# Earlier first products, joined input loads and 384/256 output pieces in a state-space and feed-forward kernel on one core

## The chip, the cores and the metric

The kernel runs on one core of a Trainium2 chip. The metric is the time of one execution on the device, in microseconds (us); less is better. A quoted time is the median of several executions, with the lowest and the highest in brackets. All times inside a trace count from the start of that execution's span; the timed execution is about 1.8 us longer than the span.

## The reference, cut to what matters

Two branches share the input `x` (2048 rows of 640 numbers, bf16) and are blended with a gate that is computed from each row.

```python
# cut: set-up of the inputs, types
x = A_x                                                   # (1, 2048, 640)
g = sigmoid((x * gate_w).sum(-1, keepdims=True))
# branch A: a diagonal complex state-space recurrence with input and output projections
Bu = einsum("bld,pd->blp", x, B_bar);  h = Lam_bar * h + Bu[:, t];  y = 2 * einsum(h, Cmat).real + x * Dskip
# branch B: a feed-forward block, 640 -> 1728 -> 640
b = gelu(x @ w1 + b1) @ w2 + b2
return g * a + (1 - g) * b
```

## The kernel before

The rows come in four chunks of 512; a chunk has four tiles of 128 rows (`TPC = 4`, `H = 2`, `P = 128`, `D = 640`). For the first chunk TensorE itself transposes `x`; the other chunks come by a transposing load. For each tile it first transposes columns 0 to 255 (I call this the tile's turn: two products against an identity matrix), and later the other 384 columns (its rest-turn: three products). The weights `w1` are split by columns into three blocks, `w1a`, `w1b` and `w1c`. The products with the first block, `w1a`, come in strips of six 128-column products, one per bank (a bank is one of the buffers that TensorE writes its products to), in between.

The first loads and their order of issue (cuts marked):

```python
load_x0(nc.sync, 0, 1, 0, KA * P)            # tile 0, columns 0..255
load_w1a(nc.scalar, 0)
load_x0(nc.sync, 1, 2, 0, KA * P)            # tile 1
load_w1a(nc.scalar, 1)
load_x0(nc.sync, 2, 3, 0, KA * P)            # tile 2
load_x0(nc.scalar, 0, H, KA * P, D)          # tiles 0 and 1, columns 256..639
load_x0(nc.sync, 3, 4, 0, KA * P)            # tile 3
load_w1a(nc.sync, 2)
# cut: two memsets on VectorE
warm = const.tile([P, 1], F32, name="warm")
nc.scalar.activation(out=warm[:], in_=nc.const_aps.tensor(1.0, [P, 1], BF16), func=ACT.Exp)
rows(nc.sync, prmA[0:KS, :], A_log_dt)       # a parameter row
rows(nc.sync, prmA[KS:2 * KS, :], A_Lambda_im)
rows(nc.sync, prmA[2 * KS:3 * KS, :], A_Lambda_re)
load_x0(nc.sync, H, TPC, KA * P, D)          # tiles 2 and 3, columns 256..639
# cut: the other weights (w1a rows 3 and 4, w1b, w1c, ...), all on nc.sync
```

TensorE's first work. The fillers multiply ones by ones and are thrown away; they are there so that the clock is raised soon.

```python
for n in (512, 512, 512, 512, 512, 512, 128, 128):
    nc.tensor.matmul(pA[:, 0:n], lhsT=ones(P), rhs=ones(n), start=True, stop=True)

def turn_first(a, other):
    t = bank()
    turn(t, 0, a, 0);          turned(nc.vector, t, 0, a, 0, 1)               # copied out by VectorE
    turn(other, a * P, a, 1);  turned(nc.scalar, other, a * P, a, 1, 2)       # copied out by ScalarE

turn_first(0, pA); turn_first(1, bank())
# cut
part(0, 0); part(0, 1)           # part(kd, a): strip kd on tile a, six products of 128 columns
turn_first(2, pA); part(1, 0); part(1, 1)
turn_first(3, pA); part(0, 2)
turn_rest(0, bank(), (nc.scalar, KA, KD)); part(1, 2)
# cut: a small product for the parameter rows, rest-turns of tiles 1, 2 and 3, all remaining strips,
# then full 512-column products with w1a, w1b, w1c
```

The down-projection of the feed-forward, whose 640 output columns the kernel spreads over two banks:

```python
MAIN, REST = (0, 512), (512, D)
# biased(): ScalarE fills a bank with the bias; two 128-column rests share a bank
# full():   13 products per tile and piece;   out_of(): ScalarE scales the piece out of the bank
```

Of the kernel before, what the change touches and what calls it, by code (L numbers as in the profile page):

```python
# [16 lines left out]
P = 128  # L17
T = 2048
D = 640
# [4 lines left out]
KS = D // P  # L24
# [3 lines left out]
TPC = CH // P  # L28
H = TPC // 2
# [12 lines left out]
def kernel(  # L42
# [19 lines left out]
    nc = tc.nc  # L62
# [12 lines left out]
    def bank(dtype=F32):  # L75
        return ps.tile([P, CH * 4 // (4 if dtype == F32 else 2)], dtype, name="bank")
# [19 lines left out]
    prmA = const.tile([P, P], BF16, name="prmA")  # L96
# [23 lines left out]
    def load_xn(c, a0=0, a1=TPC, queue=None):  # L120
        if a0 == 0:
            xn[c] = xnp.tile([P, TPC, D], BF16, name="xn")
        r0 = c * CH + a0 * P
        (queue or nc.sync).dma_start(out=xn[c][:, a0:a1, :], in_=x2d[r0:r0 + (a1 - a0) * P, :].rearrange("(a p) d -> p a d", p=P))

    def load_w1a(queue, kd):
        queue.dma_start(out=w1a[kd][:], in_=B_w1[kd * P:(kd + 1) * P, 0:cut1])

    def rows(queue, dst, v):
        queue.dma_start(out=dst, in_=v.rearrange("(j p) -> j p", p=P))  # L130

    KA = 2
    xn[0] = xnp.tile([P, TPC, D], BF16, name="xn")

    def load_x0(queue, a0, a1, d0, d1):
        queue.dma_start(out=xn[0][:, a0:a1, d0:d1], in_=x2d[a0 * P:a1 * P, d0:d1].rearrange("(a p) d -> p a d", p=P))  # L136
# [2 lines left out]
    load_w1a(nc.scalar, 0)  # L139
    load_x0(nc.sync, 1, 2, 0, KA * P)  # L140
    load_w1a(nc.scalar, 1)
    load_x0(nc.sync, 2, 3, 0, KA * P)
    load_x0(nc.scalar, 0, H, KA * P, D)
    load_x0(nc.sync, 3, 4, 0, KA * P)
    load_w1a(nc.sync, 2)
    nc.vector.memset(prmA[:], 0.0)
    nc.vector.memset(prmB[:], 0.0)
    warm = const.tile([P, 1], F32, name="warm")
    nc.scalar.activation(out=warm[:], in_=nc.const_aps.tensor(1.0, [P, 1], BF16), func=ACT.Exp)
    rows(nc.sync, prmA[0:KS, :], A_log_dt)  # L150
    rows(nc.sync, prmA[KS:2 * KS, :], A_Lambda_im)
    rows(nc.sync, prmA[2 * KS:3 * KS, :], A_Lambda_re)
    load_x0(nc.sync, H, TPC, KA * P, D)
# [36 lines left out]
    class Clock:  # L190
        pe = 3.4
        act = 12.0
# [8 lines left out]
    def let_out(until, chunk=-1):  # L201
        while pend:
            ready, cost, fn, _ = pend[0]
            start = max(ck.dve, ready)
            if start >= until and not any(x[3] == chunk for x in pend if chunk >= 0):
                return
            pend.pop(0)
            fn()
            ck.dve = start + cost
# [6 lines left out]
    def pe(cols):  # L216
        ck.pe += cols / 2400.0 + 0.002

    def act(cost):
        ck.act = max(ck.act, ck.pe + 0.2) + cost  # L220
        return ck.act
# [4 lines left out]
    nc.vector.tensor_copy(out=tf[:], in_=tfi[:])  # L226
    ones = lambda n: nc.const_aps.tensor(1.0, [P, n], BF16)
    pA = bank()
    for n in (512, 512, 512, 512, 512, 512, 128, 128):
        nc.tensor.matmul(pA[:, 0:n], lhsT=ones(P), rhs=ones(n), start=True, stop=True)  # L230

    def turn(p, col, a, kd):
        nc.tensor.matmul(p[:, col:col + P], lhsT=xn[0][:, a, kd * P:(kd + 1) * P], rhs=ident[:], start=True, stop=True,  # L233
                         skip_group_check=True)

    def turned(engine, p, col, a, k0, k1):
        dst = xT[0][:, k0:k1, a * P:(a + 1) * P]
        src = p[:, col:col + (k1 - k0) * P].rearrange("p (k t) -> p k t", t=P)
        if engine is nc.vector:
            nc.vector.tensor_copy(out=dst, in_=src)  # L240
        else:
            nc.scalar.activation(out=dst, in_=src, func=ACT.Identity)  # L242

    def turn_first(a, other):
        t = bank()
        turn(t, 0, a, 0)
        turned(nc.vector, t, 0, a, 0, 1)
        turn(other, a * P, a, 1)
        turned(nc.scalar, other, a * P, a, 1, 2)

    turn_first(0, pA)
    turn_first(1, bank())

    def col(name, dtype=F32, n=KS):
        return const.tile([P, n], dtype, name=name)
# [68 lines left out]
    banks = [bank() for _ in range(FA)]  # L324

    def strip(kd, t0, t1, first, f0=0, f1=FA):
        for kf in range(f0, f1):
            ff1_mm(banks[kf], 0, kf, kd, t0, t1, first, 3)
# [30 lines left out]
    def part(kd, a):  # L359
        strip(kd, a * P, (a + 1) * P, kd == 0)  # L360

    part(0, 0)
    part(0, 1)
    turn_first(2, pA)
    part(1, 0)
    part(1, 1)
    turn_first(3, pA)
    part(0, 2)
# [175 lines left out]
    def ssm(c, at={}):  # L544
        hs[c] = hsp.tile([P, 2 * KS, CH], BF16, name="hs")
        for ks in range(KS):
            if ks in at:
                at[ks]()
            bu = work.tile([P, 2, CH], BF16, name="bu", bufs=8)
            for ri, BT in enumerate((BT_re, BT_im)):  # L550
                p = bank()
                for kd in range(KD):
                    nc.tensor.matmul(p[:], lhsT=BT[ks >= KSA][:, kd, (ks % KSA if ks < KSA else ks - KSA) * P:][:, 0:P], rhs=xT[c][:, kd, :],  # L553
                                     start=(kd == 0), stop=(kd == KD - 1))
                    pe(CH)
                nc.scalar.activation(out=bu[:, ri, :], in_=p[:], func=ACT.Identity)  # L556
                act(0.6)
            scan_ops(c, ks, bu, ck.act)
            if c == 0 and ks == 0:
                later(0, 1.6, factors)  # L560
            let_out(ck.pe)
# [24 lines left out]
            dve_now(ck.pe, 0.45, lambda: nc.vector.tensor_tensor(out=p[:, 0:d1 - d0], in0=xn[c][:, a, d0:d1], in1=Dbc[:, d0:d1], op=ALU.mult))  # L586
            seeded[ti].append(p)

    MAIN, REST = (0, 512), (512, D)
    opened = {}  # L590

    def biased(c, kind, i):
        p = bank()
        d0, d1 = MAIN if kind == "wide" else REST
        n = 1 if kind == "wide" else H
        v, src = p[:, 0:n * (d1 - d0)], b2bc[:, d0:d1]
        if n > 1:
            v = v.rearrange("p (j d) -> p j d", j=n)
            src = src.rearrange("p (o d) -> p o d", o=1).to_broadcast([P, n, d1 - d0])
        nc.scalar.activation(out=v, in_=src, func=ACT.Identity)  # L600
        act(0.6 if n == 1 else 0.4)
        opened[c, kind, i] = p

    def first_banks(c):
        biased(c, "wide", 0)
        biased(c, "wide", 1)

    def fin_b(c, at={}):
        def full(p, col, a, d0, d1):
            for kf in range(KF - 1):  # L610
                nc.tensor.matmul(p[:, col:col + d1 - d0], lhsT=gel[c][:, kf, a * P:(a + 1) * P], rhs=w2_sb[:, kf, d0:d1],  # L611
                                 start=False, stop=False, skip_group_check=True)
                pe(d1 - d0)

        def out_of(p, col, a, d0, d1):
            ti = c * TPC + a
            if gbs[ti] is None:
                gbs[ti] = fwork.tile([P, D], F32, name="gb")
            nc.scalar.activation(out=gbs[ti][:, d0:d1], in_=p[:, col:col + d1 - d0], func=ACT.Identity, scale=gcol[:, 1, ti:ti + 1])  # L619
            act(0.7 if d1 - d0 > 320 else 0.4)  # L620

        def half_rows():
            for d0, d1 in (MAIN, REST):
                for j in range(H):
                    for h in range(2):
                        p, col = (opened[c, "wide", h * H + j], 0) if d0 == 0 else (opened[c, "rest", h], j * P)
                        nc.tensor.matmul(p[:, col:col + d1 - d0], lhsT=gelL[c % 2][h * F_LAST:(h + 1) * F_LAST, j, :],  # L627
                                         rhs=w2l[h * F_LAST:(h + 1) * F_LAST, d0:d1], start=False, stop=True, skip_group_check=True)
                    pe(d1 - d0)
            ck.pe += 0.2  # L630

        biased(c, "rest", 0)
        biased(c, "wide", 2)
        for h in range(2):
            for j in range(H):
                a = h * H + j
                full(opened[c, "wide", a], 0, a, *MAIN)
                if a == 0:
                    biased(c, "wide", 3)
                    biased(c, "rest", 1)  # L640
                if h == 1:
                    out_of(opened[c, "wide", a], 0, a, *MAIN)
                if a in at:
                    at[a]()
                let_out(ck.pe)
            for j in range(H):
                full(opened[c, "rest", h], j * P, h * H + j, *REST)
            if h == 0:
                half_rows()
                for j in range(H):  # L650
                    out_of(opened[c, "wide", j], 0, j, *MAIN)
            for j in range(H):
                out_of(opened[c, "rest", h], j * P, h * H + j, *REST)
            let_out(ck.pe)

    def fin_a(c, at={}):
# [36 lines left out]
    ssm(1, {KS - 1: lambda: first_banks(0)})  # L693
    gates(1)
    fin_b(0, {a: (lambda a=a: fold(a)) for a in range(3)})
    gel_tile(2)
    ff1(2, 0, {1: lambda: fold(3), 4: lambda: fold(4), 9: lambda: seed(0), 11: lambda: seed(1)})
# [3 lines left out]
    ssm(2, {KS - 1: lambda: first_banks(1)})  # L701
    fin_b(1, seeds(1))
    fin_a(1)
    load_xn(3)
    ssm(3)
    gel_tile(3)
    ff1(3, 0, {KF - 3: lambda: first_banks(2)})
# [36 lines left out]
```

## Time and profile before

| | value | where |
|---|---|---|
| time, first three executions | 216.24 us (216.13 to 216.39) | times |
| span of the profiled execution (itself timed at 215.6 us) | 213.8 us | the page |
| TensorE (PE) busy | 98% | the page |
| share of PE in the chain that ended last | 96% | the page |
| last PE instruction starts | 210.87 us | trace |

The lines of the page for the span, for the busy time of the engines, and for the chain of work that ended last by engine:

```profile
span 213.8 us, 3572 instructions
PE 208.6 (98%) x1384; PEld 117.0 (55%) x1403; DVE 189.1 (88%) x389; ACT 103.4 (48%) x188; POOL 1.0 (0%) x13
...
PE 96%; DMA 1%; issue 1%; SPq 0%; DVE 0%; ACT 0%
```

TensorE is the limit. VectorE (DVE) is busy for 88% but is nearly absent from the chain. A change pays only if it shortens TensorE's stream, or the few microseconds before that stream becomes dense.

The timeline of the start. Columns: start in us, length of the group in us, engine, source line, operation, operands, number of instructions; in square brackets how long the engine sat idle before and what ended that. L233 is the transposing product, L268 the product with weights.

```profile
2.14 1.28 ACT L149 ACT_TABLE_LOAD   x1 [2.14 <-issue]
3.50 0.42 PE L233 MATMUL bank<-ident,xn 128*128 128x128 bf16 x2
4.30 0.29 PE L233 MATMUL bank<-ident,xn 128*128 128x128 bf16 x2 [0.39 <-DMA xn<-in_A_x_dram]
4.42 1.08 PE L268 MATMUL bank<-xT,w1a 128*128 128x128 bf16 x12
5.34 0.28 PE L233 MATMUL bank<-ident,xn 128*128 128x128 bf16 x2
5.45 0.83 PE L268 MATMUL bank<-xT,w1a 128*128 128x128 bf16 x12
6.12 0.28 PE L233 MATMUL bank<-ident,xn 128*128 128x128 bf16 x2
6.72 0.33 PE L233 MATMUL bank<-ident,xn 128*128 128x128 bf16 x3
...
8.13 0.33 PE L233 MATMUL bank<-ident,xn 128*128 128x128 bf16 x3
```

The lines of two products are the turns of tiles 0, 1, 2 and 3; the two lines of three products are the rest-turns of tiles 0 and 2. Only tile 1's turn waits for a load here (0.39 us).

The down-projection, in the groups by shape (columns: line, engine, operation, operands, shape, count; busy us and mean ns of one; idle time before). L611 is the product, L619 the step out of the bank:

```profile
L611 PE MATMUL bank<-w_sb,gel 128*128 128x512 bf16 x200 | 45.5, 379 | 0.6 <-issue 0.3
L611 PE MATMUL bank<-w_sb,gel 128*128 128x128 bf16 x208 | 12.9, 219 | 0.0
L619 ACT ACTIVATE gb<-bank,gcol 128x512 f32<-128x512 f32 x16 | 10.5, 684 | 29.4 <-PE bank L627 17.8 <-PE bank L611 11.6
L619 ACT ACTIVATE gb<-bank,gcol 128x128 f32<-128x128 f32 x16 | 5.0, 367 | 3.2 <-PE bank L611 3.2
```

The 379 and 219 ns are lengths of pipelined products that overlap, so they can't be added. What counts is the distance from one start to the next in the trace: 216 ns for 512 columns and 56 ns for 128. (The group has 200 of 208 products: some records are missing from the trace.)

### The profile page before, as it was taken

The page shows a single profiled execution, that of the slowest core. Times are in us where ns is not written, and L with a number is a line of the kernel's source. Part 1 is how long each engine was busy: PE and PEld are TensorE (multiplying, and loading weights), DVE is VectorE, ACT ScalarE, POOL GpSimd, SP SyncE. Part 2 cuts the span into 40 slices and gives each one's busy share as a digit, 9 for nine tenths or more (in the row PEclk, how much of TensorE's full clock was granted, in tenths as well). Part 3 has the DMA queues.
Part 4 walks back from the last instruction along what each step waited for, and adds up shares of the span by engine and source line. Part 5 has one row for each costly group of instructions (what it writes and reads, how often), then busy time and mean ns, then how long its engine had stood idle before and what let it go on. Part 6 is the DMA issues. An engine that isn't in the chain of part 4 may idle for free.

```text
span 213.8 us, 3572 instructions
## 1 busy us (share of the span) xinstructions
PE 208.6 (98%) x1384; PEld 117.0 (55%) x1403; DVE 189.1 (88%) x389; ACT 103.4 (48%) x188; POOL 1.0 (0%) x13
## 2 busy tenths in 40 slices
PE   7999999999999999999999999999999999999994
PEld 3845444454454544775445577444455577664773
DVE  1599999999999999999999999999999999983153
ACT  3699956675839688203563210455683422204200
POOL 1000000000000000000000000000000000000000
PEclk9999999999999999999999999999999999999999
DMA  6869999997000000051000006100000000100011
GB/s 192 243 157 191 205 186 290 313 210 185 0 0 0 3 0 0 14 183 65 0 0 3 0 0 186 62 0 2 3 0 14 0 3 31 61 34 0 0 66 61
DMA packets 31572, 15.84 MB, mean 74 GB/s; under 512 B 22979, under 2 KB 31555, under 8 KB 31555
## 3 DMA queue, kind: packets, MB, share of 16 engines
q1 hardware_dynamic: 30850, 14.99, 28.9%
q10 hardware_dynamic: 704, 0.62, 1.0%
q8 instruction: 11, 0.18, 0.4%
q14 instruction: 7, 0.05, 0.1%
HBM read 7.48 MB, written 2.62 MB: 47 GB/s over the span
## 4 chain that ended last, share of the span: by engine, by line
PE 96%; DMA 1%; issue 1%; SPq 0%; DVE 0%; ACT 0%
PE bank L611 26%; PE bank L268 26%; PE bank L670 20%; PE bank L553 20%; DMA xn<-in_A_x_dram 1%; PE bank L627 1%; PE bank L294 1%; PE bank L233 1%; SPq L136 0%; DVE ot L675 0%; ACT xT L242 0%; PE bank L284 0%; PE bank L402 0%; PE bank L371 0%
## 5 line engine op out<-in xcount | busy, mean ns | idle before, releaser
L611 PE MATMUL bank<-w_sb,gel 128*128 128x128 bf16 (+1 forms) x408 | 57.1, 298 | 0.6 <-issue 0.3
L611 PEld LDWEIGHTS <-gel 128*128 128x128 bf16 x416 | 32.2, 98 | 25.6
L556 ACT ACTIVATE bu<-bank 128x512 bf16<-128x512 f32 x40 | 23.7, 606 | 37.3 <-PE bank L553 37.3
L273 ACT ACTIVATE gel<-bank,colB 128x512 bf16<-128x512 f32 x52 | 33.7, 695 | 11.1 <-PE bank L268 10.4
L670 PEld LDWEIGHTS <-hs 128*128 128x128 bf16 x330 | 31.5, 98 | 11.6
L507 DVE TENSOR_TENSOR_SCAN g<-r_c,carry,v 128x512 bf16<-128x512 f32 x30 | 37.3, 1269 | 0.0
L619 ACT ACTIVATE gb<-bank,gcol 128x512 f32<-128x512 f32 (+1 forms) x32 | 15.1, 526 | 32.7 <-PE bank L627 17.8
L268 PE MATMUL bank<-xT,w1a 128*128 128x512 bf16 (+1 forms) x170 | 27.6, 311 | 0.3
L670 PE MATMUL bank<-CT_im,hs 128*128 128x320 bf16 (+2 forms) x165 | 27.1, 295 | 0.0
L670 PE MATMUL bank<-CT_re,hs 128*128 128x320 bf16 (+2 forms) x165 | 27.1, 295 | 0.0
L675 DVE SCALAR_TENSOR_TENSOR ot<-bank,gcol,gb 128x320 bf16<-128x320 f32 (+2 forms) x33 | 17.4, 532 | 8.9 <-PE bank L670 8.7
L553 PE MATMUL bank<-xT,BT_im 128*128 128x512 bf16 x99 | 24.8, 379 | 0.1
L553 PE MATMUL bank<-xT,BT_re 128*128 128x512 bf16 x97 | 24.5, 379 | 0.2
L268 PEld LDWEIGHTS <-w1a 128*128 128x128 bf16 x174 | 14.1, 98 | 11.7 <-issue 0.2
L268 PE MATMUL bank<-xT,w1b 128*128 128x512 bf16 x80 | 17.9, 379 | 0.0
L586 DVE TENSOR_TENSOR bank<-xn,Dbc 128x320 f32<-128x320 bf16 (+2 forms) x33 | 14.4, 480 | 3.7 <-ACT gb L619 3.6
L553 PEld LDWEIGHTS <-BT_im 128*128 128x128 bf16 x100 | 9.8, 98 | 11.8
L488 DVE TENSOR_TENSOR v<-wa,wb 128x512 bf16<-128x512 bf16 x40 | 15.2, 420 | 0.6
L553 PEld LDWEIGHTS <-BT_re 128*128 128x128 bf16 x100 | 9.6, 98 | 11.0
L600 ACT ACTIVATE bank<-b2bc 128x512 f32<-128x512 bf16 (+1 forms) x24 | 11.7, 526 | 6.7 <-DVE ot L675 6.7
L488 DVE TENSOR_TENSOR wa<-TCOS,g 128x1024 bf16<-128x1024 bf16 x20 | 13.7, 685 | 0.1
L268 PE MATMUL bank<-xT,w1c 128*128 128x512 bf16 x57 | 13.6, 379 | 0.2
(101 smaller groups left out, 166.4 us busy)
## 6 DMA issues: line engine op xcount, KB each, us to landing
out_dram<-ot SPq DMA_DIRECT2D x15, 160.0 KB, 1.8
w_sb<-in_B_w_dram SPq DMA_DIRECT2D x1, 2080.0 KB
xn<-in_A_x_dram SPq DMA_DIRECT2D x3, 640.0 KB
w1b<-in_B_w_dram SPq DMA_DIRECT2D x5, 128.0 KB, 3.7
w1c<-in_B_w_dram SPq DMA_DIRECT2D x5, 112.0 KB, 4.4
w1a<-in_B_w_dram ACTq DMA_DIRECT2D x2, 192.0 KB, 3.3
w1a<-in_B_w_dram SPq DMA_DIRECT2D x1, 384.0 KB, 3.7
xn<-in_A_x_dram SPq DMA_DIRECT2D x4, 64.0 KB, 3.3
```

The lines of the kernel that those rows point to most:

```text
L268: nc.tensor.matmul(p[:, t0:t1], lhsT=w, rhs=xT[c][:, kd, t0:t1], start=(kd == 0) if first is None else first, stop=(kd == last), skip_grou ...
L273: nc.scalar.activation(out=gel[c][:, kf, :], in_=p[:, :], func=ACT.Gelu_apprx_tanh, bias=b1_c[:, kf:kf + 1])
L488: nc.vector.tensor_tensor(out=o, in0=a, in1=b, op=op)
L507: nc.vector.tensor_tensor_scan(s["g"][:, ri, :], r_c[:, ks:ks + 1].to_broadcast([P, CH]), s["v"][:, ri, :], init, ALU.mult, ALU.add)
L553: nc.tensor.matmul(p[:], lhsT=BT[ks >= KSA][:, kd, (ks % KSA if ks < KSA else ks - KSA) * P:][:, 0:P], rhs=xT[c][:, kd, :], start=(kd == 0 ...
L556: nc.scalar.activation(out=bu[:, ri, :], in_=p[:], func=ACT.Identity)
L586: dve_now(ck.pe, 0.45, lambda: nc.vector.tensor_tensor(out=p[:, 0:d1 - d0], in0=xn[c][:, a, d0:d1], in1=Dbc[:, d0:d1], op=ALU.mult))
L600: nc.scalar.activation(out=v, in_=src, func=ACT.Identity)
L611: nc.tensor.matmul(p[:, col:col + d1 - d0], lhsT=gel[c][:, kf, a * P:(a + 1) * P], rhs=w2_sb[:, kf, d0:d1], start=False, stop=False, skip_ ...
L619: nc.scalar.activation(out=gbs[ti][:, d0:d1], in_=p[:, col:col + d1 - d0], func=ACT.Identity, scale=gcol[:, 1, ti:ti + 1])
L670: nc.tensor.matmul(p[:, 0:d1 - d0], lhsT=hs[c][:, j, lo:lo + P], rhs=CT[:, j % KS, d0:d1], start=False, stop=(j == 2 * KS - 1), skip_group ...
L675: nc.vector.scalar_tensor_tensor(out=ot[:, d0:d1], in0=p[:, 0:d1 - d0], scalar=gcol[:, 0, ti:ti + 1], in1=gbs[ti][:, d0:d1], op0=ALU.mult, ...
```

## The change

It has two aims: to give TensorE useful work sooner in the first microseconds, and to make the pieces of the output more even (384 and 256 columns), which also evens ScalarE's steps. Its parts are: a parameter row issued from ScalarE's queue in place of SyncE's; tiles 2 and 3 in one load; strip 0 on tile 0 ahead of tile 1's turn, with four short filler products in the wait for it; all turns using the bank `pA`; the new pieces; and the last chunk's load in two halves.

```diff
     load_w1a(nc.scalar, 1)
-    load_x0(nc.sync, 2, 3, 0, KA * P)
-    load_x0(nc.scalar, 0, H, KA * P, D)
-    load_x0(nc.sync, 3, 4, 0, KA * P)
-    load_w1a(nc.sync, 2)
     nc.vector.memset(prmA[:], 0.0)
     nc.vector.memset(prmB[:], 0.0)
+    load_x0(nc.sync, H, TPC, 0, KA * P)
+    load_x0(nc.scalar, 0, H, KA * P, D)
+    load_w1a(nc.sync, 2)
+    rows(nc.scalar, prmA[0:KS, :], A_log_dt)
     warm = const.tile([P, 1], F32, name="warm")
     nc.scalar.activation(out=warm[:], in_=..., func=ACT.Exp)
-    rows(nc.sync, prmA[0:KS, :], A_log_dt)
     rows(nc.sync, prmA[KS:2 * KS, :], A_Lambda_im)
 # cut
-    for n in (512, 512, 512, 512, 512, 512, 128, 128):
+    for n in (512, 512, 512, 512, 512, 128, 128, 128):
 # cut
     turn_first(0, pA)
-    turn_first(1, bank())
 # cut
+    for _ in range(4):
+        nc.tensor.matmul(banks[0][:, 0:P], lhsT=ones(P), rhs=ones(P), start=True, stop=True, skip_group_check=True)
     part(0, 0)
+    turn_first(1, pA)
+    part(1, 0)
     part(0, 1)
     turn_first(2, pA)
-    part(1, 0)
     part(1, 1)
     turn_first(3, pA)
 # cut
-    MAIN, REST = (0, 512), (512, D)
+    WIDE = 3 * P
+    MAIN, REST = (0, WIDE), (WIDE, D)
 # cut: costs that the kernel's own ordering model assumes for ScalarE (0.6/0.4 -> 0.5/0.6, 0.7/0.4 -> 0.56/0.45),
 # and the column offset of the second rest in its bank (j * P -> j * (D - WIDE)), in four places
-    load_xn(3)
+    load_xn(3, 0, H)
+    load_xn(3, H, TPC)
```

More of the change, by code (lines that the diff above doesn't have):

```diff
@@ L600, in biased @@
         nc.scalar.activation(out=v, in_=src, func=ACT.Identity)
-        act(0.6 if n == 1 else 0.4)
+        act(0.5 if n == 1 else 0.6)
         opened[c, kind, i] = p
@@ L619, in out_of @@
             nc.scalar.activation(out=gbs[ti][:, d0:d1], in_=p[:, col:col + d1 - d0], func=ACT.Identity, scale=gcol[:, 1, ti:ti + 1])
-            act(0.7 if d1 - d0 > 320 else 0.4)
+            act(0.56 if d1 - d0 > 320 else 0.45)
         def half_rows():
@@ L625, in half_rows @@
                     for h in range(2):
-                        p, col = (opened[c, "wide", h * H + j], 0) if d0 == 0 else (opened[c, "rest", h], j * P)
+                        p, col = (opened[c, "wide", h * H + j], 0) if d0 == 0 else (opened[c, "rest", h], j * (D - WIDE))
                         nc.tensor.matmul(p[:, col:col + d1 - d0], lhsT=gelL[c % 2][h * F_LAST:(h + 1) * F_LAST, j, :],
@@ L646, in fin_b @@
             for j in range(H):
-                full(opened[c, "rest", h], j * P, h * H + j, *REST)
+                full(opened[c, "rest", h], j * (D - WIDE), h * H + j, *REST)
             if h == 0:
@@ L652, in fin_b @@
             for j in range(H):
-                out_of(opened[c, "rest", h], j * P, h * H + j, *REST)
+                out_of(opened[c, "rest", h], j * (D - WIDE), h * H + j, *REST)
             let_out(ck.pe)
```

## The prediction

> **What bounds the kernel.** TensorE. On the page PE is busy 98% of the 213.8 us span, and the chain that ended last is PE for 96%. In the timeline its matmuls run gapless from about 7 us to 211.5 us; the list of waits has no PE wait after the first load. VectorE (88%) and ScalarE (48%) have slack. So the change pays only where it shortens PE's stream or the first 7 us.
>
> **Output pieces 384/256 instead of 512/128.** The start-to-start times of the down-projection's matmuls in the trace are 216 ns (512 columns) and 56 ns (128): 272 ns for a pair, 208 pairs. The 320-column ones of the other projection take 136 ns. All are columns/2.4 GHz plus about 2.6 ns; the Trainium skill ("TensorE: Matmul & The Clock Gate", "Wait — 56ns, not 53.3ns?") states such a fixed cost of about 2.5 ns per matmul, and this trace agrees. Estimate: 162.6 + 109.3 = 272 ns. No gain. The half-row products (222 then 54 ns a pair, about 95 ns exposed before and after) sum to the same. ScalarE, from groups by shape: eviction 684 + 367 ns before; about 578 + 473 ns by interpolation; bias fills 2x596 + 385 ns against about 2x490 + 596 ns. Neutral again, and off the path. The instruction order on VectorE moves in three places (folds earlier, two seed products shifted); nothing on PE waits for these. Splitting the last input load: nothing.
>
> **Start.** Before: fillers end about 3.4 us; tile 0's first transpose 3.49; PE idle 3.7 to 4.30 for tile 1's load (landed 4.25); strip 0 on tile 0 starts 4.42, stalls 0.25 us at 4.7 for a PSUM bank, is done by 5.0. Then turn 2 at 5.33, turn 3 at 6.12, a 0.16 us bank wait, rest-turn of tile 0 at 6.72; dense afterwards.
>
> After: fillers end about 3.2, transpose about 3.33 (tile 0 landed 3.17), four cold fillers to about 3.97, strip 0 on tile 0 about 4.0 to 4.4, tile 1's turn about 4.45, strip 1 on tile 0 at 4.55 (its weights landed 4.50), done 4.9. That is 0.4 to 0.45 us ahead. It is mostly given back: strip 0 on tile 1 waits about 0.1 us for its copy (turn 4.45 + about 0.55), ends about 5.35; then turn 2 needs the joined load. Tile 2 alone landed at 4.89, tile 3 at 5.90 (15 of its 16 parts by 5.44); joined, I estimate 5.4 to 5.9, since the queue was backlogged. Then only six 56 ns matmuls stand between turns that share one bank, and turn to copied is 0.59 us, so two bank waits of about 0.15 us stand where there was one: rest-turn of tile 0 at 1.2 us after turn 2, that is 6.65 to 7.1, against 6.72. Net: -0.1 to +0.4 us. The parameter row on the other queue lets later loads issue about 0.4 us sooner, but PE waits for none of them: its next ones had slack.
>
> **Prediction.** 216.15 us; 8 in 10 between 215.6 and 216.7. Faster by over 2%: 0.5%; within 2%: 98.5%; slower: 1%.
>
> **Checks in the profile.** Start-to-start 162 to 163 and 109 ns for the new pieces; first strip matmul near 4.0 us; turn 2 waiting for the joined load; two bank waits before the rest-turn of tile 0, at 6.6 to 7.1 us; the first 512-column products within 0.4 us of before's; the stretches from 57 us on equal in length.
>
> **What would make it wrong.** The joined load landing as early as tile 2 alone (then 0.3 us gained) or later than 6 us (a real loss); a different moment of clock release, now at about 4.1 us; 384- or 256-column products with another fixed cost (5 ns each would be 2 us); VectorE's new order delaying a bank that PE needs.

## More of the kernel before

In the chain that ended last, the second chunk's down-projection reads so (start, length, what):

```profile
108.29 0.22 PE bank L611
...
123.17 10.87 PE bank L670 x80
```

From the first of its products to the first product of the next stage it takes 123.17 - 108.29 = 14.88 us.

## The result, and the profile after

The changed kernel takes **216.03 us** (215.62 to 216.39, 6 runs) against **216.09 us** (215.83 to 216.39, 6 runs) for the kernel before. The ratio is 0.9997, with a 95% interval of 0.9981 to 1.0012. A ratio is the mean time of one kernel's fast runs over that of the other's fast runs of the same rounds, so it is not quite the ratio of the medians. Nothing moved that can be resolved. What has to be explained is where the earlier start went, and whether the zero is one cause or several that cancel.

The same lines of the page:

```profile
span 214.4 us, 3599 instructions
PE 210.3 (98%) x1407; PEld 125.9 (59%) x1407; DVE 189.1 (88%) x389; ACT 103.1 (48%) x188; POOL 1.0 (0%) x13
...
PE 96%; DMA 2%; SPq 0%; DVE 0%; issue 0%
```

The start (L232 transposes, L361 is a filler, L239 copies a transposed piece out of its bank, L266 is a product with weights):

```profile
2.83 1.28 ACT L149 ACT_TABLE_LOAD   x1 [2.83 <-issue]
3.46 0.39 PE L232 MATMUL bank<-ident,xn 128*128 128x128 bf16 x2
3.64 0.63 PE L361 MATMUL bank<-const-bfloat16-1.0 128*128 128x128 bf16 x4
3.78 0.29 DVE L239 CAST xT<-bank 128x128 bf16<-128x128 f32 x1 [2.35 <-PE bank L232]
4.12 0.51 PE L266 MATMUL bank<-xT,w1a 128*128 128x128 bf16 x6
4.47 0.28 PE L232 MATMUL bank<-ident,xn 128*128 128x128 bf16 x2
4.59 0.98 PE L266 MATMUL bank<-xT,w1a 128*128 128x128 bf16 x12
6.04 0.29 PE L232 MATMUL bank<-ident,xn 128*128 128x128 bf16 x2 [0.47 <-DMA xn<-in_A_x_dram]
...
6.65 0.27 PE L232 MATMUL bank<-ident,xn 128*128 128x128 bf16 x2
...
7.25 0.33 PE L232 MATMUL bank<-ident,xn 128*128 128x128 bf16 x3
...
8.79 0.34 PE L232 MATMUL bank<-ident,xn 128*128 128x128 bf16 x3
```

Strip 0 on tile 0 does start 0.30 us sooner (4.12 against 4.42). Then tile 2's turn waits for the joined load: in the trace that load lands at 5.99, and the turn is at 6.04 against 5.34 before, where tile 2 alone had landed at 4.89. Between that turn and the rest-turn of tile 0 the new order is quicker, 7.25 - 6.04 = 1.21 us against 6.72 - 5.34 = 1.38. From there to the rest-turn of tile 2 it is slower, 8.79 - 7.25 = 1.54 us against 8.13 - 6.72 = 1.41, because that rest-turn waits for its own load (columns 256 to 639 of tiles 2 and 3), which landed at 8.74, against 7.75 before. The sum is 0.70 - 0.17 + 0.13 = 0.66 us; the first product with `w1b` starts at 13.092 against 12.447 us, 0.65 later.

The down-projection, by shape, and its stretch of the chain:

```profile
L613 PE MATMUL bank<-w_sb,gel 128*128 128x384 bf16 x208 | 35.2, 327 | 0.0
L613 PE MATMUL bank<-w_sb,gel 128*128 128x256 bf16 x208 | 24.0, 273 | 0.0
L621 ACT ACTIVATE gb<-bank,gcol 128x384 f32<-128x384 f32 x16 | 8.8, 577 | 23.8 <-PE bank L629 16.3 <-PE bank L613 7.4
L621 ACT ACTIVATE gb<-bank,gcol 128x256 f32<-128x256 f32 x16 | 6.7, 474 | 9.2 <-PE bank L613 9.2
```

```profile
108.94 7.06 PE bank L613 x52
...
123.82 10.87 PE bank L672 x80
```

The stretch is again 123.82 - 108.94 = 14.88 us. The starts are 162.5 ns apart for 384 columns and 109.2 ns for 256 (means without the few larger gaps), which is 271.7 ns for a pair against 215.8 + 55.8 = 271.6 before.

So in this pair of profiles the start costs 0.65 us, while the medians agree to 0.06 us. Two readings are possible. Either the profiled executions are not typical of the timed ones, or something pays the loss back. The experiments were built to find out which.

My theory: (1) the pieces are neutral; (2) the new order is slightly quicker; (3) the loads take that back, and more; (4) the moment at which the clock of TensorE is raised differs from one execution to the next, and decides how much of this is visible. The rivals: the pieces gain something that the start loses; or the new order itself costs time through its bank waits.

### The profile page after: what moved, and what is told of

Same layout as the page of the kernel before. It is cut to its first block, busy times and chain, and to the rows that moved or that the text cites. A ratio compares the mean times of both kernels' runs of the same rounds, so it can differ in the third digit from the quotient of the medians.

```text
span 214.4 us, 3599 instructions
## 1 busy us (share of the span) xinstructions
PE 210.3 (98%) x1407; PEld 125.9 (59%) x1407; DVE 189.1 (88%) x389; ACT 103.1 (48%) x188; POOL 1.0 (0%) x13
## 4 chain that ended last, share of the span: by engine, by line
PE 96%; DMA 2%; SPq 0%; DVE 0%; issue 0%
PE bank L613 27%; PE bank L266 26%; PE bank L672 20%; PE bank L554 20%; DMA xn<-in_A_x_dram 2%; PE bank L629 1%; PE bank L292 1%; PE bank L232 1%; SPq L136 0%; DVE ot L677 0%; PE bank L282 0%; PE bank L403 0%; PE bank L372 0%
## 5 line engine op out<-in xcount | busy, mean ns | idle before, releaser
L613 PE MATMUL bank<-w_sb,gel 128*128 128x384 bf16 (+1 forms) x416 | 57.9, 300 | 0.0
L613 PEld LDWEIGHTS <-gel 128*128 128x128 bf16 x416 | 40.3, 98 | 17.1 <-issue 0.8
L621 ACT ACTIVATE gb<-bank,gcol 128x384 f32<-128x384 f32 (+1 forms) x32 | 15.1, 526 | 33.0 <-PE bank L613 16.6
L266 PE MATMUL bank<-xT,w1a 128*128 128x512 bf16 (+1 forms) x174 | 28.0, 313 | 0.0
L266 PEld LDWEIGHTS <-w1a 128*128 128x128 bf16 x174 | 14.3, 98 | 11.6
L266 PE MATMUL bank<-xT,w1b 128*128 128x512 bf16 x80 | 17.9, 379 | 0.0
L602 ACT ACTIVATE bank<-b2bc 128x384 f32<-128x384 bf16 (+1 forms) x24 | 11.7, 528 | 7.7 <-DVE ot L677 7.7
L266 PE MATMUL bank<-xT,w1c 128*128 128x512 bf16 x60 | 13.7, 379 | 0.0
```

The costliest lines, as they stand in the source:

```text
L266: nc.tensor.matmul(p[:, t0:t1], lhsT=w, rhs=xT[c][:, kd, t0:t1], start=(kd == 0) if first is None else first, stop=(kd == last), skip_grou ...
L602: nc.scalar.activation(out=v, in_=src, func=ACT.Identity)
L613: nc.tensor.matmul(p[:, col:col + d1 - d0], lhsT=gel[c][:, kf, a * P:(a + 1) * P], rhs=w2_sb[:, kf, d0:d1], start=False, stop=False, skip_ ...
L621: nc.scalar.activation(out=gbs[ti][:, d0:d1], in_=p[:, col:col + d1 - d0], func=ACT.Identity, scale=gcol[:, 1, ti:ti + 1])
```

## The experiments

All twelve kernels gave correct results. Within one call all kernels ran on the same chip, in turn with the kernel before.

### First call: one part at a time

`e1_pieces_only`: the kernel before with the new pieces alone.

```diff
-    MAIN, REST = (0, 512), (512, D)
+    MAIN, REST = (0, 3 * P), (3 * P, D)      # and the four offsets and two assumed costs of the change
```

> Only the 384/256 output pieces, on the kernel before; start and loads untouched. My theory (a fixed 2.6 ns per matmul, so pieces are neutral): starts 162 and 109 ns apart, about 7.06 us and 7.17 us for the two halves of the down-projection, time within 0.15% of before. Rival (the pieces cost what the start gains): slower than before by 0.2 to 0.5 us, and PE waits appear in the down-projection. First rest-turn of tile 0 at about 6.7 us as before.

Measured: 215.98 us (215.39 to 216.13), ratio to the kernel before 1.0006 [0.9987, 1.0026].

`e3_loads_as_before`: the changed kernel with the loads of the kernel before. The two parts, join and row, were undone together: with two loads and the row left on ScalarE's queue, the row would have waited there for the first weight load. (Not tried, but the traces show the reason: the ninth load of a program reuses the semaphore, that is the completion counter, of the first weight load, and is issued just after that has landed, at 3.46 us after 3.38 in before and at 3.69 after 3.61 in after.)

```diff
-    load_x0(nc.sync, H, TPC, 0, KA * P)
+    load_x0(nc.sync, 2, 3, 0, KA * P)
+    load_x0(nc.sync, 3, 4, 0, KA * P)
-    rows(nc.scalar, prmA[0:KS, :], A_log_dt)
+    rows(nc.sync, prmA[0:KS, :], A_log_dt)       # after the warming activation, as before
```

> The kernel after, but with the loads of before: two loads for tiles 2 and 3, the parameter row back on SyncE's queue. New order of turns and strips and the fillers kept. My theory (the joined load gives the start's gain back): turn 2 no longer waits for its load and runs at about 5.4 to 5.5 us, instead of 6.04; the rest-turn of tile 0 at 6.6 to 6.9 us instead of 7.25, set now by bank waits and by tile 3's landing (about 5.9); span about 0.4 us shorter than that of the changed kernel, so about 0.1 to 0.2% faster than it. Rival (the order of turns and its bank waits give it back): rest-turn stays at 7.1 us or later.

Measured: 215.95 us (215.39 to 216.34), ratio 1.0009 [0.9989, 1.0029].

`e5_order_as_before`: the changed kernel with the old fillers and the old order of turns and strips.

```diff
-    for n in (512, 512, 512, 512, 512, 128, 128, 128):
+    for n in (512, 512, 512, 512, 512, 512, 128, 128):
     turn_first(0, pA)
+    turn_first(1, bank())
-    for _ in range(4): ...                       # the four short fillers
     part(0, 0)
-    turn_first(1, pA)
-    part(1, 0)
     part(0, 1)
     turn_first(2, pA)
+    part(1, 0)
     part(1, 1)
```

> The kernel after, but with the old fillers and the old order of turns and strips; new loads and pieces kept. My theory: strip 0 on tile 0 back at about 4.4 us; turn 2 still waits for the joined load (landing 5.6 to 6.0) where the old order wants it at about 5.3; twelve products then stand between turns 2 and 3, so one bank wait only; rest-turn of tile 0 at landing plus 1.4 us, about 7.1 to 7.4. So as slow as the changed kernel or up to 0.2 us slower. Rival (the loads are harmless, the order costs): rest-turn at 6.7 us as before.

Measured: 216.25 us (215.48 to 217.96), ratio 1.0035 [1.0000, 1.0069]; one of its six runs, at 217.96, stretches the interval.

`e6_two_banks`: a candidate. It has the old loads and the new order, but the two products of a turn go into one bank, and the turns take two banks alternately, so that a turn need not wait for the copy of the turn just before it.

```diff
-    def turn_first(a, other):
-        t = bank()
+    def turn_first(a, t):                        # t alternates: pA, second, pA, second
         turn(t, 0, a, 0)
+        turn(t, P, a, 1)
         turned(nc.vector, t, 0, a, 0, 1)
-        turn(other, a * P, a, 1)
-        turned(nc.scalar, other, a * P, a, 1, 2)
+        turned(nc.scalar, t, P, a, 1, 2)
```

> A candidate: loads of before, new order and fillers, and each tile's two turns go to one PSUM bank, alternating between two banks, so that no turn waits for the copy of the turn just before. My theory: no bank wait of 0.15 us between turn 2 and the rest-turn of tile 0, which comes at about 6.4 us (tile 3's landing near 5.9 sets it); prmA product at about 6.9 instead of 7.22; span 0.3 us below before, time about 0.15% faster than before. Rival (the end is not set by the start): the rest-turn moves, the span does not.

Measured: 216.45 us (215.75 to 216.73), ratio 1.0027 [1.0006, 1.0049]. Its interval lies just above 1: it is no gain, and if anything slower by some 0.3%.

The kernel before had a median of 215.51 us on this chip, and its 11 runs fall in two clusters, six at 215.25 to 215.51 and five at 216.04 to 216.45. That spread, 1.2 us, is larger than all that I wanted to tell apart, so the times alone decide nothing about the start. The expectations for single events at the start can't be judged as written either. In `e3_loads_as_before` the rest-turn of tile 0 came at 7.42 us, which by the letter meets the rival's "7.1 us or later", and in `e6_two_banks` at 7.58 where 6.4 was expected; but in both TensorE was still slow when the start came (below). Only `e5_order_as_before` went as expected: the joined load landed at 5.68, the turn of tile 2 followed at 5.72, and the rest-turn of tile 0 came at 7.12. The traces decide two things.

**The pieces are neutral, and the rest of the kernel is fixed.** From the start of the first `w1b` product to the last PE instruction, the traces of the three kernels with 512/128 pieces (before, and two more below) all show 198.42 us; those of all others, with 384/256 pieces, show 198.33 us. The pieces gain 0.09 us, 0.04% of the time. Within each group this length agrees to 0.01 us, whatever the start was. Set beside the time of the very execution that was profiled:

| kernel | clock raised, us | first `w1b` product, us | time of that run, us | difference, us |
|---|---|---|---|---|
| before | 4.10 | 12.45 | 215.60 | 203.15 |
| after | 4.19 | 13.09 | 216.18 | 203.09 |
| e5_order_as_before | 5.16 | 12.84 | 215.94 | 203.10 |
| e3_loads_as_before | 6.34 | 13.15 | 216.34 | 203.19 |
| e1_pieces_only | 6.37 | 13.04 | 216.13 | 203.09 |
| e6_two_banks | 6.98 | 13.35 | 216.52 | 203.17 |

In these six profiles the whole kernel is the moment of the first `w1b` product plus 203.1 to 203.2 us. Apart from the 0.09 us of the pieces, every difference between them is made before that product.

**The clock is raised at another moment in each execution, and this moves the start.** The start of `e1_pieces_only` is instruction for instruction that of the kernel before. Its timeline:

```profile
4.25 1.49 PE L268 MATMUL bank<-xT,w1a 128*128 128x128 bf16 x12
5.53 0.42 PE L233 MATMUL bank<-ident,xn 128*128 128x128 bf16 x2
5.74 1.14 PE L268 MATMUL bank<-xT,w1a 128*128 128x128 bf16 x12
6.72 0.28 PE L233 MATMUL bank<-ident,xn 128*128 128x128 bf16 x2
...
7.32 0.33 PE L233 MATMUL bank<-ident,xn 128*128 128x128 bf16 x3
```

The rest-turn of tile 0 is at 7.32 us against 6.72, although its loads landed sooner than in the profile of before (tile 2 at 4.71 against 4.89, tile 3 at 5.53 against 5.90). The difference is the clock: until 6.37 us a 128-column product took 107 ns in place of 56, so that twelve of them take 1.49 and 1.14 us where before has 1.08 and 0.83. Here PE waits for no load after tile 1's, because it is too slow to need one. In this pair the late clock thus costs 0.6 us and at the same time hides waits for loads. This also swamps the comparison that I wanted from `e3_loads_as_before`: in its trace tile 2 had landed at 4.82 but its turn came only at 6.13, held by slow products.

The Trainium skill ("TensorE: Matmul & The Clock Gate", "What's actually happening") describes this: activity is judged in free-running windows of 3413 ns that do not restart with the kernel. The traces agree. The stretches at full clock in their records are multiples of 3.413 us (for example 6.83, 208.21 and 211.63 us: 2, 61 and 62 windows). The same page says that the transition point varies by about 500 ns from run to run (section "What you observe"); here the six profiles above, whose first filler starts at 0.77 us in all, spread over 2.9 us (4.10 to 6.98, that is 3.3 to 6.2 us after that filler).

### Second call: the start held back until the clock is up

To take the clock out of the comparison, I held the first loads back behind ten VectorE products, with fillers on TensorE in the meantime, in four versions: the kernel before, the changed kernel, the changed kernel with the old loads, and the candidate.

```diff
+    # dum: 128x640 f32; all in program order, SyncE too
+    nc.vector.memset(dum[:], 0.0)
+    for _ in range(10):
+        nc.vector.tensor_tensor(out=dum[:], in0=dum[:], in1=dum[:], op=ALU.mult)
+    nc.vector.tensor_copy(out=xn[0][:, 0, 0:1], in_=dum[:, 0:1])    # the first loads overwrite these columns,
+    nc.vector.tensor_copy(out=w1a[0][:, 0:1], in_=dum[:, 0:1])      # so they wait, and the result stays correct
+    nc.vector.tensor_copy(out=gate[:], in_=dum[:, 0:P])
 # the fillers become 22 products of 512 columns on ones and 9 that wait for gate
```

> The kernel before, with the whole start held back about 9 us behind a fixed chain of ten VectorE products, while TensorE runs fillers, so that its clock has been released before any load is issued (the five other profiles so far show the release anywhere from 4.1 to 6.9 us). My theory (the moment of release makes the scatter of the times and swamped the last four runs): release between 4.1 and 7.6 us, all strips at 56 ns, and the six times of this run within 0.4 us of each other, against 1.2 us for before in the last job. Rival (the landing of the loads scatters): as wide as before. Rest-turn of tile 0 about 6.0 us after the first load is issued, as in the first profile of before.

> The kernel after, held back the same way. My theory (with a released clock the joined load is waited for): tiles 2 and 3 land 5.0 to 5.3 us after the first load's issue, turn 2 right then, rest-turn of tile 0 at 6.2 to 6.5 us after it; span and median time 0.2 to 0.5 us above those of the held-back before. Rival (nothing is given back): 0.2 us or more below it. If pieces or the rest cost anything, the distance from the first 512-column product to the end differs by more than 0.1 us; I expect less.

> The new order with the loads of before, held back the same way. My theory (the joined load is the loss): turn 2 at 4.6 to 4.9 us after the first load's issue, not waiting for a load; rest-turn of tile 0 at 5.8 to 6.1; median time 0.3 us or more below the held-back after, and 0 to 0.2 us below the held-back before. Rival (the two bank waits are the loss): as slow as the held-back after.

> The candidate with two banks in turn and the loads of before, held back the same way. My theory: no bank waits, the rest-turn of tile 0 at 5.4 to 5.8 us after the first load's issue, the product on the parameter rows about 0.3 us earlier than in the held-back before; median time 0.2 to 0.4 us below it. Rival (a later stage, not the start, sets the end): same time as the held-back before.

Measured: `w_before` 225.47 us (224.92 to 225.69), `w_after` 225.60 (225.03 to 226.07), `w_loads_as_before` 226.15 (224.99 to 226.18), `w_two_banks` 225.00 (224.64 to 226.04). The aim was missed, and a look at `w_after` in three stretches shows why (columns: stretch, its length and the busy time of each engine with its count, the granted clock, the DMA share and GB/s):

```profile
6.80:10.50 3.70, 0.37 (x2) 0.00 (x0) 3.56 (x8) 0.00 (x0) 0.00 (x0) 1.00 0.00 0
10.55:13.95 3.40, 3.39 (x8) 1.20 (x9) 0.22 (x4) 1.49 (x2) 0.00 (x0) 0.50 0.70 214
14.00:17.00 3.00, 2.90 (x43) 2.44 (x42) 0.97 (x4) 0.87 (x4) 0.00 (x0) 1.00 0.97 291
```

The fillers were done too early. No product started on TensorE between 6.79 and 10.56 us (the record of the last one ends at 7.17), and the clock was taken back to 0.50 for exactly one window, just when the start came. The same befell the profiled execution of `w_loads_as_before`, but not those of the other two, whose clock had been raised later (5.35 and 6.33 us). So these four can't be compared as four. The record shows how it went in the timed runs, for it lists the mean granted clock of each: 0.992 where such a window fell inside (half a clock for 3.4 of 224 us), 1.000 elsewhere. It is 0.992 in 2 of 5 runs of `w_before`, 2 of 6 of `w_after`, 5 of 6 of `w_loads_as_before` and 1 of 5 of `w_two_banks`; the runs of one kernel that have it are 0.4 to 1.1 us slower in the mean than its others (226.12 against 224.99 us for `w_loads_as_before`). So the clock does move the time by that much. Among the runs at 1.000, `w_after` has a mean of 225.33 us (4 runs) and `w_before` 225.14 (3), too few and too near to tell apart. The clean pair in it, `w_before` and `w_two_banks`, has the rest-turn of tile 0 at 5.79 and 5.55 us after the issue of the first load, and the first `w1b` product at 11.52 and 11.33.

### Third call: the fillers paced, so that the clock stays up

The same idea with the hole filled: seven steps of two VectorE products each, and after each step five filler products that wait for it. The clock was raised at 5.8 to 7.6 us and never taken back; the loads began at 13.4 us.

```diff
+    for i in range(8):
+        if i == 7:                       # now the first loads may start
+            nc.vector.tensor_copy(out=xn[0][:, 0, 0:1], in_=TSIN[:, 0, 0:1])
+            nc.vector.tensor_copy(out=w1a[0][:, 0:1], in_=TSIN[:, 0, 0:1])
+        nc.vector.tensor_copy(out=gate[i][:], in_=TSIN[:, 0, 0:P])
+        for _ in range(6 if i == 7 else 5):
+            nc.tensor.matmul(held[:, 0:512], lhsT=gate[i][:], rhs=ones(512), start=True, stop=True)
+        if i < 7:
+            for _ in range(2):
+                nc.vector.tensor_tensor(out=dum, in0=dum, in1=dum, op=ALU.mult)      # dum = TSIN[:, 0:2, :]
 # the old fillers are gone; the rest as in the four kernels
```

> Second try at holding the start back with a released clock. In the first try the fillers ended up to 4 us before the first load and two of four traces show the clock withdrawn again for one 3.41 us period just then, so those two cannot be compared. Now fillers are paced by the VectorE chain, five per 1.5 us, to the end. This is the kernel before. My theory: clock released at 4.1 to 7.6 us and never withdrawn; rest-turn of tile 0 at 5.7 to 6.0 us after the first load's issue (5.79 in the first try's clean trace); times within 0.5 us of each other.

> The kernel after, held back with a released clock. My theory (the joined load is waited for): tiles 2 and 3 land 4.6 to 5.3 us after the first load's issue, turn 2 right after, rest-turn of tile 0 1.2 us after turn 2, at 5.85 to 6.5; time 0 to 0.5 us above the held-back before. Rival (nothing given back): at least 0.2 us below it. Pieces: from the first product of the second weight block to the end within 0.1 us of the held-back before.

> New order, loads of before, held back. My theory (joined load costs up to what it lands late): tile 2 lands 0.3 to 0.9 us sooner than joined, turn 2 at 4.4 to 4.8 after the first load's issue, then bank waits set the pace: rest-turn of tile 0 at 5.6 to 6.0; time 0.2 us or more below the held-back after and within 0.2 us of the held-back before. Rival (bank waits alone are the loss): equal to the held-back after.

> Two banks in turn, loads of before, held back. The first try's clean trace had the rest-turn at 5.55 and the last output 0.28 us earlier than the held-back before. My theory: rest-turn at 5.3 to 5.6 us after the first load's issue, no bank wait; time 0.2 to 0.4 us below the held-back before. Rival (no difference): within 0.1 us.

| kernel | median (range), us | mean, us | runs | first `w1b` product in its profile, us |
|---|---|---|---|---|
| x_before | 228.07 (227.99 to 228.25) | 228.09 | 4 | 25.09 |
| x_after | 228.82 (228.56 to 228.89) | 228.77 | 4 | 25.38 |
| x_loads_as_before | 228.10 (227.85 to 228.29) | 228.12 | 5 | 24.98 |
| x_two_banks | 228.43 (227.74 to 228.90) | 228.33 | 5 | 24.46 |

With the clock up, `x_before` scatters by 0.26 us and `x_after` by 0.33 in four runs each, where the kernel before had 0.96 us in nine runs on the same chip (1.2 on the chip of the first call, 2.3 on that of the second). Fewer runs scatter less by themselves, and `x_two_banks` still has 1.16. Now the change shows: `x_after` is 228.77 - 228.09 = 0.68 us slower than `x_before` (0.3%), and the ranges don't overlap. That is more than the 0 to 0.5 us that was expected. With the loads put back, the new order and the new pieces take the time of `x_before` (228.12 against 228.09). So the loads (the join and the row together), not the order, cost the time. This is a statement about the held-back start; the order's own gain is not visible in these times.

What the loads do, in the timelines. `x_before`, the turn of tile 2 and the rest-turns of tiles 0, 1 and 2:

```profile
17.97 0.29 PE L246 MATMUL bank<-ident,xn 128*128 128x128 bf16 x2 [0.21 <-DMA xn<-in_A_x_dram]
...
19.36 0.33 PE L246 MATMUL bank<-ident,xn 128*128 128x128 bf16 x3
...
20.27 0.33 PE L246 MATMUL bank<-ident,xn 128*128 128x128 bf16 x3
...
20.77 0.33 PE L246 MATMUL bank<-ident,xn 128*128 128x128 bf16 x3
```

`x_after`, the same four; for the last, the loading of its weights (PEld), which names the wait:

```profile
17.98 0.29 PE L245 MATMUL bank<-ident,xn 128*128 128x128 bf16 x2
...
19.19 0.33 PE L245 MATMUL bank<-ident,xn 128*128 128x128 bf16 x3
...
20.10 0.33 PE L245 MATMUL bank<-ident,xn 128*128 128x128 bf16 x3
...
21.07 0.17 PEld L245 LDWEIGHTS <-xn 128*128 128x128 bf16 x3 [0.49 <-DMA xn<-in_A_x_dram]
```

`x_loads_as_before`, the rest-turns of tiles 0 and 2:

```profile
19.25 0.33 PE L246 MATMUL bank<-ident,xn 128*128 128x128 bf16 x3
...
20.66 0.33 PE L246 MATMUL bank<-ident,xn 128*128 128x128 bf16 x3
```

In this execution of `x_after` the joined load came as early as tile 2 alone in `x_before` and in `x_loads_as_before` (4.54 us after the first issue against 4.53 and 4.56), where 0.3 to 0.9 us between them had been expected, and the new order was 0.17 us ahead at the rest-turn of tile 0. Then the rest-turn of tile 2 waited for its load and the lead became a lag: 21.08 against 20.77 us. With the old loads the same order is 0.11 us ahead at both places. This profiled pair differs by 0.31 us in time and the means by 0.68, so this wait explains about half of the mean difference directly; I have no trace of the slower executions of `x_after`.

Over all traces, times after the issue of the first load:

- The joined load landed at 4.54 to 5.27 us (four traces, mean 4.83). Tile 2 alone landed at 3.92 to 4.56 (ten traces, mean 4.21), tile 3 alone at 4.54 to 5.20 (mean 4.90). Joined, both tiles come when the later one came before, and the first is 0.6 us late.
- The load for the rest-turns of tiles 2 and 3 landed at 6.74 to 8.02 us (four traces with the new loads, mean 7.3), against 6.43 to 7.03 (mean 6.6) with the old ones, although it was issued sooner (3.29 to 3.64 against 3.55 to 4.06). A load tells its landing in sixteen shares. With the new loads fifteen of them were in by 5.95 to 6.19 us in three traces (7.14 in the fourth), somewhat sooner than with the old ones (6.16 to 6.51); the last share came 0.7 to 1.7 us behind, its packets mostly one per 33 ns. With the old loads it was at most 0.65 us behind.

Whether the join or the row on the other queue makes that share late was not separated, and why it trails is open.

The candidate isn't proven. Its rest-turn came at 5.34 us after the first issue, as expected, but the time did not follow: 0.2 to 0.4 us below `x_before` were expected. Its profiled run was its fastest (227.74 us), but its other four lie at 228.13 to 228.90, and its mean is above that of `x_before`. Its scatter also remained wide with the clock up, so the clock is not the only source of scatter. No version here is shown to beat both kernels.

## Why the prediction was right, and where it was not

The time was right: 216.15 us predicted, 216.03 measured, in the range, and "within 2%" was given 98.5%. That the number came so near is in part luck: it stands at the fast end of the prediction's own net of -0.1 to +0.4 us, if that is counted from the 216.24 us before, while the profiled pair lost 0.65 us at the start and the held-back pair 0.68. Point by point:

- **TensorE is the limit; the pieces cost nothing. Right, and shown.** 162.6 and 109.3 ns were predicted, 162.5 and 109.2 measured. From the first `w1b` product to the last PE instruction it is 198.33 us in eleven traces with the new pieces, against 198.42 in three with the old ones. The fixed cost of about 2.5 ns per product that the Trainium skill states ("TensorE: Matmul & The Clock Gate", "Wait — 56ns, not 53.3ns?") held for two widths that the down-projection before did not have. ScalarE's steps came at 577 and 474 ns where 578 and 473 were predicted.
- **The stretches later on equal in length. Right.** 14.88 us in both for the second chunk's down-projection. Nothing came of VectorE's new order or of the last load in two halves.
- **First strip product near 4.0 us. Nearly: 4.12.** The load of tile 0 landed at 3.41 us, not at 3.17 as in the profile of before, so that the first transposing product came at 3.46 where 3.33 was predicted; the strip then waited for VectorE's copy, which ended at 4.07. Issuing the row took 0.64 us of ScalarE's queue and moved its table load from 2.14 to 2.83 and its first copy from 3.95 to 4.23, but this strip does not read that copy: with the row back on SyncE (`e3_loads_as_before`) it also starts 0.67 us after the first transposing product, against 0.66.
- **Tile 2's turn waits for the joined load. Right; its size was too small.** I estimated a landing at 5.4 to 5.9 us; it was 5.99.
- **Two bank waits before the rest-turn of tile 0. Right:** two gaps of 210 ns between starts where 56 is normal, about 0.15 us each. The rest-turn itself was at 7.25 us, outside the 6.6 to 7.1 that I gave.
- **"The parameter row on the other queue lets later loads issue about 0.4 us sooner, but PE waits for none of them: its next ones had slack". Wrong: this is the step that failed.** They issued about 0.2 us sooner (4.37 against 4.57 for the rest of tiles 2 and 3; the rows ahead of it on SyncE still had to wait for the first weights, which landed at 3.61 against 3.38), and that very load landed a microsecond later, at 8.74 us, past the moment when PE wanted it.
- **"The first 512-column products within 0.4 us of before's". Wrong in the profiled pair: 0.65 us.** The terms were sized too small: the joined load 0.70 us, of which the new order gave 0.17 back, plus 0.13 for the load that I had said cost nothing.
- **"A different moment of clock release" was named as a risk but not priced.** It turned out to be as large as everything that the change does: 0.6 us between two executions with the same start.

Why is the loss of 0.65 us in one pair of profiles not in the medians? The profiled execution of before was faster than all six of its timed runs (215.6 against 215.83 to 216.39), while that of after lay in the middle of its own (216.18 in 215.62 to 216.39). Both had the clock early, at 4.1 and 4.2 us, and that is where a late load shows most. With a late clock, TensorE is too slow to need the loads, as `e1_pieces_only` and `e3_loads_as_before` show for the old loads; no trace has the changed kernel with a late clock. The timed runs probably mix both cases. That this mixture brings the loss to nothing in the medians is argued from these traces, not shown run by run, as a timed run leaves no trace. The interval still allows a difference of -0.2% to +0.1%, so the 0.3% of the held-back start is not hidden in it: something in the ordinary start takes it back or keeps it from arising.

## What to carry to other kernels

Before judging a change of half a microsecond at the start of a kernel, find out how widely that start scatters by itself, and if the clock is the source, compare with the clock already up: here the scatter of one of the kernels fell from 0.96 to 0.26 us (in fewer runs), and a difference of 0.3% became visible that six ordinary runs did not show. Be wary of joining two loads when the consumer needs the first part alone: over these traces both parts then arrived when the later one had. The Trainium skill has the other side of this ("Perfetto Trace Analysis", "DMA Optimizations"): where the DMA engines are generally idle, splitting "may allow some to start sooner". Here they were busy (their mean busy share from 4 to 5 us is about 1.0 before and after), and the first tile still landed 0.6 us sooner in the mean when it came alone. What the join by itself costs in time was not measured.

## What the Trainium skill lacked or had wrong

- "TensorE: Matmul & The Clock Gate": the section "What you observe" has the transition around 4 us, give or take 500 ns from run to run. Six profiles of kernels with nearly the same fillers show 4.10 to 6.98 us, 3.3 to 6.2 us after the first filler. The free-running window of 3413 ns that the page describes is in line with the traces and already implies a spread of up to a window. The page's "What's actually happening" puts the cost of the ramp below 1% of a typical span; that holds here, some 0.6 us of 216, but it is as large as the change that was to be judged. The page does not say that a late clock also hides waits for loads.
- "TensorE: Matmul & The Clock Gate", "What's actually happening": that an idle window brings the slow clock back fits two traces: 3.77 us without the start of a product, over a whole window (7.15 to 10.56 in `w_after`), cost one window at 0.50, while two other kernels with 3.0 us (7.58 to 10.56) and 2.5 us (8.05 to 10.56), which cover no whole window, kept their clock. But a whole window is not needed: at the end of `e5_order_as_before` the last product starts at 211.17 us, and the clock is down again at 213.38, 2.2 us later.
- "DMA: Bandwidth & Descriptors", "Issuing engines are not separate DMA queues": it says that issuing on several engines saves only the sequencer's time to initiate the transfer, usually small. It does not say that this time is charged to the other engine's own work: a row of parameters took 0.64 us of ScalarE's queue, which delayed its table load by 0.69 us (no product waited for that here), while SyncE's later loads were issued only 0.2 us sooner.
- "DMA: Bandwidth & Descriptors", "Latency and other measured facts": it says that two of the sixteen DMA engines are usually slower than the others and gives a guess at the cause that holds for loads issued from GpSimd alone. These loads are issued from SyncE, and one share of sixteen still trailed: it was 0.7 to 1.7 us behind the other fifteen with the new loads and set the landing of the whole, 6.74 to 8.02 us after the first issue against 6.43 to 7.03 with the old. Which engine it was, the traces do not say.
